# A split-float32 chain of products on one core: stationary operands laid out with a step of two, moving operands of three products read backwards

## Chip, cores and metric

The kernel runs on 1 core of a Trainium2 chip. The metric is the device time of one execution in microseconds; the median of three runs stands for the kernel. Engines are named as the profile names them: PE (TensorE, its matmuls), PEld (its weight loads), DVE (VectorE), ACT (ScalarE), POOL (GpSimd), SP (the queue that issues most transfers).

## What is computed

Three layers follow each other; batch 8, sequence 576, width 512, inner width 1024, all float32 (the weights of the feed-forward parts come as 64-bit floats and are brought to float32 on the chip).

```
q_s = softmax(q, -1);  k_s = softmax(k, over the sequence)
x   = q_s @ (k_s^T @ v)                                # linear attention, 8 heads of 64
gate = sigmoid(causal 5-tap convolution of x);  val = x @ w_val
y   = (gate * val) @ w_out
xk  = mu_k * y + (1 - mu_k) * y_prev;  xr likewise with mu_r
k   = relu(xk @ w_k);  v = (k * k) @ w_v;  r = sigmoid(xr @ w_r)
out = r * v
```

## The kernel before, in words

The 8 x 576 rows of the sequence are cut into 12 tiles of 384 columns (`T`), and features lie on the 128 partitions. Tile i goes through the steps V (`val`, with W_val), Y (`y`, W_out), R (`r`, W_r), and H and A alternating (`hid`, W_k; `vacc`, W_v): eight H steps, each A step three H steps behind its own (`LAG`, line 59). In V, Y and H a 128 x 128 block of the weight is the stationary operand and an activation of 384 columns the moving one (`product`, line 568). In R and A the roles are turned: a 128-column part of the activation is stationary and 512 columns of the weight move (lines 628 and 652).

Tile 0 multiplies in plain float32, and each of its products has two records in the trace. From tile 1 on, every operand a is split into a rounded part "hi" and a remainder "lo" in the format float32r (`split`, line 439: ACT casts the hi part, DVE subtracts for the lo part), and each product becomes three: hi x hi, and hi x lo and lo x hi (`passes`, line 446). Weights are split once, chunk by chunk, between tiles 0 and 1 (`split_weight`, line 228: ACT writes hi at line 240, DVE writes lo at line 241). The squared hidden activations are split by `hid` (lines 641 to 644) into a pair of tiles `kh`, `kl`, from eight buffers of one tag.

Every product has a weight load of its own; the load of the next product is recorded while the present one streams. In the compiled program of this kernel, each weight load is written with the address of its last column and a step of minus one element; each moving operand and each output has a step of plus one.

The order of the work is written out by hand: `FRONT` (line 22) for the first tiles, and from tile 2 on one side step list `REST` (line 38) that places the next tile's attention, convolution and rounds of k and v behind numbered steps of the present tile. The pads `LEFT_GAP` and `RIGHT_GAP` (line 56) shift where the pools lie.

Of the kernel before, what the change touches and what calls it, by code (L numbers as in the profile page):

```python
# [9 lines left out]
F32R = mybir.dt.float32r  # L10
# [56 lines left out]
def tile_linear_attention_gated_conv_channel_mix(  # L67
# [15 lines left out]
    nc = tc.nc  # L83
    B, H, S, D = q.shape
    DM = H * D
# [3 lines left out]
    P = 128  # L89
    NC = DM // P  # L90
    NF = DFF // P
    T = 384
# [9 lines left out]
    WC = 512  # L102
# [5 lines left out]
    work = ctx.enter_context(tc.tile_pool(name="work", bufs=1))  # L108
    gatep = ctx.enter_context(tc.tile_pool(name="gated", bufs=1))
# [17 lines left out]
    def f32(ap):  # L127
        return ap.bitcast(F32)
# [15 lines left out]
    def scratch(name):  # L144
        return work.tile([P, T], F32, tag="m", bufs=4, name=name)
# [43 lines left out]
    def tap(c, t):  # L189
# [6 lines left out]


    HALF = ("wout", "wv")
    SHAPES = {"wval": (w_val, DM, DM), "wout": (w_out, DM, DM), "wr": (w_r, DM, DM), "wk": (w_k, DM, DFF), "wv": (w_v, DFF, DM)}
    CHUNKS = {  # L200
        f"{w}{x}": (w, at) for w, (_, rows, width) in SHAPES.items()
        for x, at in enumerate((kc, c0) for c0 in range(0, width, WC) for kc in range(rows // P))
    }
    PLACES = len(CHUNKS) + 1
    raws, whole, upper, lower = {}, {}, {}, {}

    def place(dtype, name):
        return wts.tile([P, WC], dtype, tag="w", bufs=PLACES, name=name)

    def load_weight(n):  # L210
        w, (kc, c0) = CHUNKS[n]
        here = n in LEFT_WEIGHTS
        raw = raws[n] = (first if here else early).tile([P, WC, 2], U32, tag="raw", bufs=1 if here else 6, name="raw")
        nc.sync.dma_start(raw.rearrange("p n w -> p (n w)"), SHAPES[w][0][kc * P:(kc + 1) * P, 2 * c0:2 * (c0 + WC)])

# [5 lines left out]
    def open_upper():  # L221
        pool = ctx.enter_context(tc.tile_pool(name="upper", bufs=1))
        for w in ("wk", "wv"):
            _, rows, width = SHAPES[w]
            t = pool.tile([P, rows // P, width], F32R, name=f"{w}_hi")
            upper.update({(w, kc): t[:, kc, :] for kc in range(rows // P)})

    def split_weight(n):
        w, (kc, c0) = at = CHUNKS[n]
        if (w, kc) not in upper:  # L230
            if w in ("wk", "wv"):
                first_ctx.close()
                open_upper()
            else:
                pair = early.tile([P, 2, WC], F32R, tag="raw", bufs=6, name=f"{w}_hi")
                upper.update({(w, kc // 2 * 2 + x): pair[:, x, :] for x in range(2)})
        h, t = upper[w, kc][:, c0:c0 + WC], whole[at]
        l = lower[at] = place(F32R, "lower")
        scale = 0.5 if w in HALF else 1.0
        nc.scalar.activation(h, t, AF.Copy, scale=scale)  # L240
        nc.vector.scalar_tensor_tensor(out=l, in0=t, scalar=scale, in1=f32(h), op0=ALU.mult, op1=ALU.subtract)

    def weight(i, w, kc, c0, n):

        at = w, (kc, c0 // WC * WC)
        o = c0 % WC
        if i == 0:
            return (whole[at][:, o:o + n],)
        return upper[w, kc][:, c0:c0 + n], lower[at][:, o:o + n]


    kvs = []
# [178 lines left out]
    def pair_of(tag, bufs, pool=work):  # L431
        return lambda name: tuple(pool.tile([P, T], F32R, tag=tag, bufs=bufs, name=name + x) for x in "hl")

    x_pair, g_pair, q_pair, k_pair = pair_of("x", 8), pair_of("g", 8, gatep), pair_of("q", 2), pair_of("k", 8)

    def one(tag, bufs, name):
        return (gatep if tag == "g" else work).tile([P, T], F32, tag=tag, bufs=bufs, name=name)

    def split(a, pair):

        nc.scalar.copy(pair[0], a)  # L441
        nc.vector.tensor_sub(pair[1], a, f32(pair[0]))  # L442
        return pair

    def passes(po, left, right, start, stop, turn=False):

        m = ((0, 0),) if len(left) == 1 else ((0, 0), (0, 1), (1, 0)) if turn else ((0, 0), (1, 0), (0, 1))
        for x, (a, b) in enumerate(m):
            nc.tensor.matmul(  # L449
                po, lhsT=left[a], rhs=right[b], start=start and x == 0, stop=stop and x == len(m) - 1  # L450
            )

    def padded(i, h, tag, bufs, name, pool=odd):

# [41 lines left out]
    def x_chunk(st, i, c):  # L496
        segs = segments(i)
        g = len(segs)
        px = ps_w.tile([P, 512], F32, tag="w", name="px")
        for o, n, b, s in segs:  # L500
            kv = (kvf[b],) if i < 2 else kvs[b % 2]
            passes(px[:, o:o + n], tuple(a[:, c, :] for a in kv), tuple(a[:, o:o + n] for a in st["q", c]), True, True)
        xv = padded(i, HALO, "xf", 2, "xf") if i else padded(i, HALO, "xf", NC, "xf", first)
        data = xv[:, :, HALO:]
        fill_past(i, xv, tail_x[:, c, :])
        nc.scalar.copy(data, px[:, :T].rearrange("p (g t) -> p g t", g=g))
        keep_tail(i, xv, tail_x[:, c, :])
        st["xv", c] = xv
        if i == 0:
            st["x", c] = (xv[:, 0, HALO:],)  # L510
            return
        xh, xl = st["x", c] = x_pair("x")
        gx = lambda a: a.rearrange("p (g t) -> p g t", g=g)
        nc.scalar.copy(gx(xh), data)
        nc.vector.tensor_sub(gx(xl), data, gx(f32(xh)))
# [38 lines left out]
    def main_steps(i, xs):  # L554
# [3 lines left out]
        st = {}  # L558
        gx = lambda a: a.rearrange("p (g t) -> p g t", g=g_n)

        def bank(pool, tag, name):
            return pool.tile([P, 512], F32, tag=tag, name=name)
# [4 lines left out]

        def product(po, w, at, acts):
            for c, a in enumerate(acts):
                passes(po, weight(i, w, c, at, P), a, c == 0, c == NC - 1)  # L570

        def row(po, w, c, a):

            for m in range(NC):
                passes(po[m][:, :T], weight(i, w, c, m * P, P), a, c == 0, c == NC - 1)

        def val(m):
            if i == 0:
                if m == 0:
                    st["pv"] = four("pv")  # L580
                row(st["pv"], "wval", m, xs["x", m])
                return
            pv = bank(ps_w, "w", "pv")
            product(pv[:, :T], "wval", m * P, [xs["x", c] for c in range(NC)])
            gated(m, pv)
# [8 lines left out]
        def y(c):  # L594
            if i == 0:
                if c == 0:
                    st["py"] = [bank(ps_w, "w", "py") if m < 2 else bank(ps_acc, "acc", "py") for m in range(NC)]
                row(st["py"], "wout", c, st["g", c])
                return
            py = bank(ps_w, "w", "py")  # L600
            product(py[:, :T], "wout", c * P, [st["g", m] for m in range(NC)])
            keep_y(c, py)
# [18 lines left out]
        def part(pair, t):  # L621
            return tuple(a[:, t * P:(t + 1) * P] for a in pair)

        def r(c):
            if c == 0:
                st["r"] = [bank(ps_acc, "acc", f"racc{t}") for t in range(NT)]
            for t in range(NT):
                passes(st["r"][t], part(st["xr", c], t), weight(i, "wr", c, 0, DM), c == 0, c == NC - 1, True)

        def rsig():  # L630
            for t in range(NT):
# [6 lines left out]
        def hid(f):  # L638
            ph = bank(ps_w, "w", "ph")
            product(ph[:, :T], "wk", f * P, [st["xk", c] for c in range(NC)])  # L640
            rf = one("k", 8, "rf") if i == 0 else scratch("rf")
            nc.scalar.activation(rf, ph[:, :T], AF.Relu)  # L642
            nc.scalar.activation(rf, rf, AF.Square)
            st["k", f] = (rf,) if i == 0 else split(rf, k_pair("k"))

        def vacc(fs, ts):

            if fs[0] == 0:
                st["v"] = [bank(ps_acc, "acc", f"vacc{t}") for t in range(NT)]
            for f in fs:  # L650
                for t in ts:
                    passes(st["v"][t], part(st["k", f], t), weight(i, "wv", f, 0, DM), f == 0, f == NF - 1, True)
            if fs[-1] == NF - 1 and len(ts) == NT:
                for t in ts:
                    finish(t)

        def finish(t):
            rs = st["rs", t]
            nc.vector.scalar_tensor_tensor(
                out=rs, in0=rs, scalar=1.0 if i else 0.0, in1=st["v"][t], op0=ALU.add, op1=ALU.mult  # L660
            )
            r0 = i * T + t * P
            nc.sync.dma_start(out[r0:r0 + P, :], rs)
# [85 lines left out]
    for n in CHUNKS:  # L749
        todo_front["l" + n] = lambda n=n: load_weight(n)  # L750
        todo_front[n] = lambda n=n: decode_weight(n)
        todo_front["s" + n] = lambda n=n: split_weight(n)
# [55 lines left out]
```

## Time and profile before

| | us |
|---|---|
| median of 3 runs | 812.47 (812.2 to 812.85) |
| span of the profiled execution | 810.1 |
| first split product (tile 1, step V) | 106.84 after the start |
| last product | 805.90 |

The profiled execution's span runs from its first instruction to its last; the median of the runs is 2.3 us longer. The page gives busy shares of engines, a picture of the span in 40 slices, and the chain of work that ended last. PE's busy time is modelled and matmuls overlap in it (one of 384 columns is recorded as 0.34 us long, while the next starts 0.17 us after it), so the pace of the products is read from starts, or from the chain, which counts each piece once.

### The profile page before, as it was taken

What the parts mean: (1) busy time and instruction counts of PE and PEld (TensorE: products, weight loads), DVE (VectorE), ACT (ScalarE), POOL (GpSimd) and SP (SyncE); (2) the same over time, 40 slices, a digit from 0 to 9 for tenths busy, and PEclk for the clock granted to TensorE, in tenths of its full rate; (3) what the DMA queues carried; (4) which work ended last, traced back from release to release, by engine and by line L of the source; (5) the groups of instructions that cost most, each with busy time, mean ns of one, the idle gap of its engine ahead of it and who ended that gap; (6) DMA issues with size and microseconds to landing.
All of it is one profiled execution on the core that took longest, in us unless ns stands there. A gap on an engine that the chain in (4) does not pass through costs nothing.

```text
span 810.1 us, 12242 instructions
## 1 busy us (share of the span) xinstructions
PE 798.3 (99%) x4578; PEld 701.2 (87%) x4578; DVE 564.5 (70%) x1016; ACT 479.3 (59%) x948; POOL 59.2 (7%) x224
## 2 busy tenths in 40 slices
PE   6999999999999999999999999999999999999998
PEld 5545588999999999989989999999999999998996
DVE  7999889976777577577758577577576747644611
ACT  4667678637746746655754763763764674664542
POOL 2130001000002001000000100100000100100000
PEclk9999999999999999999999999999999999999999
DMA  9786220132222102013041211211222010000001
GB/s 310 244 269 217 59 78 1 40 98 59 75 63 59 40 27 72 7 36 91 7 98 46 53 40 39 60 39 40 59 65 73 1 37 23 22 1 14 26 1 40
DMA packets 92537, 53.25 MB, mean 66 GB/s; under 512 B 74018, under 2 KB 84286, under 8 KB 92478
## 3 DMA queue, kind: packets, MB, share of 16 engines
q1 hardware_dynamic: 92432, 52.44, 22.3%
q8 instruction: 36, 0.59, 0.3%
q14 instruction: 23, 0.19, 0.1%
q10 hardware_dynamic: 46, 0.02, 0.0%
HBM read 43.02 MB, written 9.44 MB: 65 GB/s over the span
## 4 chain that ended last, share of the span: by engine, by line
PE 95%; DMA 2%; DVE 1%; ACT 1%; SPq 1%; issue 0%; ACTq 0%
PE ph L449 25%; PE vacc L449 25%; PE racc L449 12%; PE pv L449 12%; PE py L449 12%; PE px L449 4%; PE kvacc L347 2%; PE pq L476 2%; DMA raw<-in_moe_w_val_dram 1%; DMA raw<-in_moe_w_k_dram 1%; DVE gate L548 1%; DMA kt<-in_k_dram 1%; PE mx L333 0%; PE pmT L321 0%; SPq L303 0%; DVE whole L152 0%
## 5 line engine op out<-in xcount | busy, mean ns | idle before, releaser
L548 DVE SCALAR_TENSOR_TENSOR gate<-xf,cw,gate 128x384 f32<-128x384 f32 x192 | 117.2, 615 | 5.1 <-ACT gate L546 2.3
L449 PE MATMUL ph<-xkh,wk_hi 128*128 128x384 f32 x352 | 120.3, 342 | 0.0
L449 PE MATMUL ph<-xkl,wk_hi 128*128 128x384 f32 x352 | 118.3, 336 | 0.0
L449 PE MATMUL ph<-xkh,lower 128*128 128x384 f32 x352 | 118.1, 336 | 0.0
L642 ACT ACTIVATE rf<-ph 128x384 f32<-128x384 f32 x96 | 46.8, 488 | 99.0 <-PE ph L449 98.1
L449 PE MATMUL vacc<-wv_hi,kh 128*128 128x512 f32 x264 | 104.0, 394 | 0.0
L449 PE MATMUL vacc<-lower,kh 128*128 128x512 f32 x264 | 103.2, 391 | 0.0
L449 PE MATMUL vacc<-wv_hi,kl 128*128 128x512 f32 x264 | 103.1, 391 | 0.0
L442 DVE TENSOR_TENSOR kl<-rf,kh 128x384 fp32r<-128x384 f32 x88 | 48.9, 556 | 70.1 <-ACT kh L441 69.1
L616 DVE SCALAR_TENSOR_TENSOR xm<-yf,mus,xm 128x384 f32<-128x384 f32 x96 | 56.5, 614 | 24.2 <-ACT xm L615 23.7
L449 PEld LDWEIGHTS ph<-xkh,wk_hi 128*128 128x128 f32 x352 | 66.2, 188 | 2.0 <-ACT xkh L441 0.2
L449 PEld LDWEIGHTS ph<-xkh,lower 128*128 128x128 f32 x352 | 66.2, 188 | 1.9
L449 PEld LDWEIGHTS ph<-xkl,wk_hi 128*128 128x128 f32 x352 | 66.1, 188 | 0.0
L494 DVE TENSOR_TENSOR ql<-pq,qh 128x384 fp32r<-128x384 f32 x40 | 22.2, 556 | 62.5 <-ACT qh L493 62.5
L441 ACT CAST gh<-gf 128x384 fp32r<-128x384 f32 x44 | 22.5, 511 | 72.0 <-DVE gf L589 72.0
L449 PE MATMUL py<-gh,wout_hi 128*128 128x384 f32 x176 | 59.6, 343 | 0.0
L449 PE MATMUL pv<-xh,lower 128*128 128x384 f32 x176 | 59.5, 338 | 0.0
L449 PE MATMUL pv<-xh,wval_hi 128*128 128x384 f32 x176 | 59.5, 338 | 0.0
L449 PE MATMUL pv<-xl,wval_hi 128*128 128x384 f32 x176 | 59.3, 337 | 0.0
L449 PEld LDWEIGHTS vacc<-wv_hi,kl 128*128 128x128 f32 x264 | 49.5, 188 | 11.0 <-DVE kl L442 0.3
L449 PE MATMUL py<-gl,wout_hi 128*128 128x384 f32 x176 | 58.2, 339 | 0.0
L449 PE MATMUL py<-gh,lower 128*128 128x384 f32 x176 | 58.0, 338 | 0.0
(132 smaller groups left out, 1723.0 us busy)
## 6 DMA issues: line engine op xcount, KB each, us to landing
out_dram<-rs SPq DMA_DIRECT2D x36, 256.0 KB, 2.0
kt<-in_k_dram SPq DMA_DIRECT2D x16, 512.0 KB, 4.5
qt<-in_q_dram SPq DMA_DIRECT2D x29, 256.0 KB, 3.4
vt<-in_v_dram SPq DMA_DIRECT2D x56, 128.0 KB, 3.6
raw<-in_moe_w_k_dram SPq DMA_DIRECT2D x8, 512.0 KB, 5.5
raw<-in_moe_w_v_dram SPq DMA_DIRECT2D x8, 512.0 KB, 6.8
raw<-in_moe_w_val_dram SPq DMA_DIRECT2D x4, 512.0 KB, 6.3
raw<-in_moe_w_out_dram SPq DMA_DIRECT2D x4, 512.0 KB, 8.4
```

Source lines behind the costliest of these rows:

```text
L347: nc.tensor.matmul(acc[e * D:(e + 1) * D, x * VW:(x + 1) * VW], lhsT=kt[:, 2 * x + e, s, :], rhs=st["v"][:, 2 * x + e, s, :], start=(s == ...
L441: nc.scalar.copy(pair[0], a)
L442: nc.vector.tensor_sub(pair[1], a, f32(pair[0]))
L449: nc.tensor.matmul(po, lhsT=left[a], rhs=right[b], start=start and x == 0, stop=stop and x == len(m) - 1)
L476: nc.tensor.transpose(pq[:, t * P:(t + 1) * P], qt[:, t, 2 * c:2 * c + 2, :].rearrange("p h d -> p (h d)"), f32(ident))
L494: nc.vector.tensor_sub(ql, pq[:, :T], f32(qh))
L548: nc.vector.scalar_tensor_tensor(out=gx(gate), in0=xv[:, :, HALO - sh:HALO - sh + L], scalar=tap(c, HALO - sh), in1=gx(gate), op0=ALU.mult ...
L616: nc.vector.scalar_tensor_tensor(out=gx(xf), in0=yv[:, :, 1:], scalar=mu[:, c:c + 1], in1=gx(xf), op0=ALU.mult, op1=ALU.add)
L642: nc.scalar.activation(rf, ph[:, :T], AF.Relu)
```

## The change

Four things are altered, all for tiles 1 to 11; tile 0 keeps its products.

The split weights of W_val, W_out and W_k (`WOVEN`) keep their places in memory, but the 512 columns of a chunk are stored woven: column n of the first 256 lies at element 2n, column 256 + n at element 2n + 1. ACT and DVE write them so (lines 240 and 241, once), and a stationary block of 128 columns is then read with a step of two elements.

The pair `kh`, `kl` of the squares becomes one tile of 2T elements with hi in the even and lo in the odd elements, four buffers in place of eight. ACT writes hi and DVE writes lo with a step of two, and A's stationary blocks are read with a step of two. In tile 0 the same buffers hold two unsplit squares each, one behind the other.

The moving operands of the products with W_val, W_k and W_v (`BACK`) are read from the last column to the first, and the output in PSUM is written from the last column to the first as well, so that the result lies as before. W_out's and W_r's products keep their direction.

R's stationary operand stays dense.

```diff
+    BACK = ("wval", "wk", "wv")
+    WOVEN = ("wval", "wout", "wk")
+
+    def woven(a):
+
+        return a.rearrange("p (n e) -> p e n", e=2)
...
         scale = 0.5 if w in HALF else 1.0
+        if w in WOVEN:
+            h, l, t = woven(h), woven(l), t.rearrange("p (e n) -> p e n", e=2)
         nc.scalar.activation(h, t, AF.Copy, scale=scale)
...
-        return upper[w, kc][:, c0:c0 + n], lower[at][:, o:o + n]
+        pair = upper[w, kc][:, c0 - o:c0 - o + WC], lower[at]
+        if w in WOVEN:
+            return tuple(woven(a)[:, o // (WC // 2), o % (WC // 2):o % (WC // 2) + n] for a in pair)
+        return tuple(a[:, o:o + n] for a in pair)
...
+    def k_tile():
+        return work.tile([P, 2 * T], F32R, tag="k", bufs=4, name="k")
+
+    def k_pair():
+        t = k_tile().rearrange("p (t e) -> p e t", e=2)
+        return tuple(t[:, e, :] for e in range(2))
...
-    def passes(po, left, right, start, stop, turn=False):
+    def passes(po, left, right, start, stop, turn=False, back=False):
 
         m = ((0, 0),) if len(left) == 1 else ((0, 0), (0, 1), (1, 0)) if turn else ((0, 0), (1, 0), (0, 1))
+        back = back and len(left) > 1
+        o = po[:, ::-1] if back else po
         for x, (a, b) in enumerate(m):
-            nc.tensor.matmul(
-                po, lhsT=left[a], rhs=right[b], start=start and x == 0, stop=stop and x == len(m) - 1
-            )
+            r = right[b][:, ::-1] if back else right[b]
+            nc.tensor.matmul(o, lhsT=left[a], rhs=r, start=start and x == 0, stop=stop and x == len(m) - 1)
...
-                passes(po, weight(i, w, c, at, P), a, c == 0, c == NC - 1)
+                passes(po, weight(i, w, c, at, P), a, c == 0, c == NC - 1, back=w in BACK)
...
-            rf = one("k", 8, "rf") if i == 0 else scratch("rf")
+            if i:
+                rf = scratch("rf")
+            else:
+                if f % 2 == 0:
+                    st["rf"] = f32(k_tile())
+                rf = st["rf"][:, f % 2 * T:(f % 2 + 1) * T]
             nc.scalar.activation(rf, ph[:, :T], AF.Relu)
             nc.scalar.activation(rf, rf, AF.Square)
-            st["k", f] = (rf,) if i == 0 else split(rf, k_pair("k"))
+            st["k", f] = (rf,) if i == 0 else split(rf, k_pair())
...
-                    passes(st["v"][t], part(st["k", f], t), weight(i, "wv", f, 0, DM), f == 0, f == NF - 1, True)
+                    passes(st["v"][t], part(st["k", f], t), weight(i, "wv", f, 0, DM), f == 0, f == NF - 1, True, "wv" in BACK)
```

## Rows read from the trace of the kernel before

**Rows 1.** The page: engines, granted clock by slice, shares of the chain.

```profile
PE 798.3 (99%) x4578; PEld 701.2 (87%) x4578; DVE 564.5 (70%) x1016; ACT 479.3 (59%) x948; POOL 59.2 (7%) x224
PEclk9999999999999999999999999999999999999999
PE 95%; DMA 2%; DVE 1%; ACT 1%; SPq 1%; issue 0%; ACTq 0%
```

**Rows 2.** The chain, last tile, split products: start us, us, engine, output, count.

```profile
747.97 8.34 PE pv L449 x48
756.31 8.47 PE py L449 x48
764.78 8.17 PE racc L449 x36
...
781.25 2.08 PE ph L449 x12
783.33 2.05 PE vacc L449 x9
```

**Rows 3.** The chain, tile 0, plain float32 products, two records each.

```profile
88.36 2.58 PE ph L449 x8
...
91.92 2.58 PE vacc L449 x6
```

**Rows 4.** Groups of instructions, PE: output<-operands, shapes, count, busy us, mean ns.

```profile
L449 PE MATMUL ph<-xkh,wk_hi 128*128 128x384 f32 x352 | 120.3, 342 | 0.0
L449 PE MATMUL vacc<-wv_hi,kh 128*128 128x512 f32 x264 | 104.0, 394 | 0.0
L449 PE MATMUL py<-gh,wout_hi 128*128 128x384 f32 x176 | 59.6, 343 | 0.0
L449 PE MATMUL pv<-xh,lower 128*128 128x384 f32 x176 | 59.5, 338 | 0.0
```

**Rows 5.** The timeline, PE, narrow split products of x: start us, us recorded.

```profile
465.94 0.25 PE L449 MATMUL px<-qh,kv_hi 128*128 128x192 f32 x1
466.02 0.28 PE L449 MATMUL px<-qh,kv_lo 128*128 128x192 f32 x1
466.14 0.28 PE L449 MATMUL px<-ql,kv_hi 128*128 128x192 f32 x1
466.25 0.27 PE L449 MATMUL px<-qh,kv_hi 128*128 128x192 f32 x1
466.36 0.27 PE L449 MATMUL px<-qh,kv_lo 128*128 128x192 f32 x1
466.47 0.28 PE L449 MATMUL px<-ql,kv_hi 128*128 128x192 f32 x1
```

**Rows 6.** ACT's copies with stepped and with dense reads, and the split: ns min/median/max.

```profile
L488 ACT COPY q<-pq x4: 458/478/486, 17.2 to 29.3; 128x384 f32<-128x384 f32 x4
...
L486 ACT COPY q<-pq x4: 478/480/485, 85.8 to 101.6; 128x384 f32<-128x384 f32 x4
...
L441 ACT CAST kh<-rf x88: 498/514/536, 139.4 to 801.0; 128x384 fp32r<-128x384 f32 x88
L442 DVE TENSOR_TENSOR kl<-rf,kh x88: 547/557/562, 139.9 to 801.5; 128x384 fp32r<-128x384 f32 x88
```

**Rows 7.** Windows: step V in tiles 3, 4 and 10, then H and A in tile 7 (busy us).

```profile
236.68:245.25 8.57, 8.57 (x52) 8.54 (x50) 8.57 (x17) 1.56 (x3) 1.06 (x2) 1.00 0.24 92
300.68:309.46 8.78, 8.78 (x54) 8.70 (x53) 8.44 (x18) 2.07 (x4) 1.03 (x1) 1.00 0.23 91
686.34:694.66 8.32, 8.32 (x49) 8.32 (x48) 6.53 (x12) 2.06 (x4) 0.50 (x1) 1.00 0.25 97
...
520.38:556.88 36.50, 36.50 (x193) 33.48 (x192) 23.20 (x36) 22.39 (x46) 0.48 (x3) 1.00 0.10 22
```

**Rows 8.** The timeline, the last H's squares and the A products that wait for them.

```profile
801.52 0.56 DVE L442 TENSOR_TENSOR kl<-rf,kh 128x384 fp32r<-128x384 f32 x1 [3.57 <-ACT kh L441]
801.54 0.19 PEld L449 LDWEIGHTS vacc<-wv_hi,kh 128*128 128x128 f32 x1 [0.28 <-ACT kh L441]
...
802.14 0.30 PEld L449 LDWEIGHTS vacc<-wv_hi,kl 128*128 128x128 f32 x2 [0.30 <-DVE kl L442]
```

More of the change, by code (lines that the diff above doesn't have):

```diff
@@ L432, in pair_of @@
         return lambda name: tuple(pool.tile([P, T], F32R, tag=tag, bufs=bufs, name=name + x) for x in "hl")
-    x_pair, g_pair, q_pair, k_pair = pair_of("x", 8), pair_of("g", 8, gatep), pair_of("q", 2), pair_of("k", 8)
+    x_pair, g_pair, q_pair, k_pair = pair_of("x", 8), pair_of("g", 8, gatep), pair_of("q", 2), None
+    def k_tile():
[3 more added lines that the diff above has]
+        return tuple(t[:, e, :] for e in range(2))
     def one(tag, bufs, name):
@@ L627, in r @@
             for t in range(NT):
-                passes(st["r"][t], part(st["xr", c], t), weight(i, "wr", c, 0, DM), c == 0, c == NC - 1, True)
+                passes(st["r"][t], part(st["xr", c], t), weight(i, "wr", c, 0, DM), c == 0, c == NC - 1, True, "wr" in BACK)
         def rsig():
```

## The prediction

> **What bounds the kernel now.** I read the page first: PE is busy for 99% of the span, 95% of the chain that ended last is PE, and PE's granted clock is in the top tenth in every slice [rows 1], which is its upper level of 2.4 GHz. So no wait, transfer or clock decides; the number of products and the time from one product to the next do. That pace is read next, from the chain of the last tile, which nothing interrupts [rows 2]: V takes 8.34 / 48 = 173.8 ns a product, Y 8.47 / 48 = 176.5, R 8.17 / 36 = 226.9, H 2.08 / 12 = 173.3, A 2.05 / 9 = 227.8. At 2.4 GHz and one column a cycle 384 columns are 160.0 ns and 512 are 213.3; the two widths confirm it, since 226.9 - 173.3 = 53.6 ns for 128 more columns. So each split product pays about 13.3 ns beside its columns, at either width. Then tile 0 as the control [rows 3]: a plain float32 record takes 2.58 / 8 = 322.5 ns for 384 columns and 2.58 / 6 = 430 for 512, that is two cycles a column and 2.5 to 3.3 ns beside them. Plain products have a weight load each, as split ones do. Some 10.8 ns a product (13.3 - 2.5) therefore come only where columns stream at full pace.
>
> **What these 10.8 ns may be.** No row names them. What changes between the two is how densely the moving operand is read while the next weights are loaded. The narrow products of x show the load's own pace [rows 5]: at 192 columns (80 ns of streaming) starts lie 0.11 to 0.12 us apart, so a load takes about 110 ns for 128 elements, half the pace of a moving operand. Loads walk downwards through memory and moving operands upwards, as the compiled program has it. With the change the moving operand of V, H and A walks downwards too, and the load covers two elements of memory for each one that it takes: both then walk in one direction at one pace. If the 10.8 ns are the two streams getting in each other's way where they pass in the same part of the memory, V, H and A lose most of them. Y gets the step of two without the turn and keeps opposite directions.
>
> **The change part by part.** Counts from [rows 4], three groups a product: V 528, Y 528, H 1056, A 792; R is left alone.
>
> Pace of V, H and A: between 0 and 10.8 ns less a product if the change helps (the floor is the plain product's 2.5 ns), up to 10.8 more if the doubled reach of the load doubles the meetings. I take two thirds, 7.2 ns: the one place where the trace shows less than the usual 13 ns is the first narrow product behind a wide one, 0.08 us between starts against 80 ns of columns [rows 5], some 6 ns or less, which is nearer to two thirds gone than to nothing or all. V and H: 1584 x 7.2 = 11.4 us. A: 792 x 7.2 = 5.7 us.
>
> Pace of Y: one of the two conditions is met, so half of that, 3.6 ns (bounds 10.8 more to 10.8 less): 528 x 3.6 = 1.9 us.
>
> Writes with a step of two by ACT and DVE: weights once (16 of 28 chunks), squares 88 times. No row shows such a write. The nearest is ACT's copy that reads with a step of 128 elements: 478 ns, against 480 for the dense one of the same shape [rows 6]. I take nothing from there; the other end is a doubling (less than dense is excluded, as the dense writes run at the same pace as all others of their width). Doubled, kh and kl would add 0.51 and 0.56 us eight times a tile in a stage where DVE is busy 23.2 and ACT 22.4 of 36.5 us [rows 7], with A three H steps behind: hidden but in the last tile, where the chain would end 1.1 us later.
>
> One tile for kh and kl: a product that reads kh might now wait for kl as well. With three H steps between, that is hidden in every tile but the last, where PE already waits 0.28 us for kh and 0.30 us for kl [rows 8]; there it costs at most the two kh products that now run ahead, 0.46 us. The buffers hold as many squares as before, so none comes free later. No DMA moves.
>
> Given back: PE getting faster meets DVE in V. In eight of the eleven tiles (1 and 3 to 9) DVE is busy for nearly the whole of V, as in the first two windows of [rows 7]; in three it has 2 us to spare, as in the third. In the eight, V's 48 x 7.2 = 0.35 us may turn into a wait of Y for the gated activations: 8 x 0.35 = 2.8 us, and 0.3 for the end.
>
> Sum: 11.4 + 5.7 + 1.9 - 3.1 = 15.9 us. The profiled span of 810.1 becomes 794.2; the runs' median lies 2.3 us above the span, so 812.5 - 15.9 = **796.6 us**.
>
> **The rivals.**
> All of it goes: V, H, A and Y fall to the plain product's 2.5 ns: 2904 x 10.8 = 31.4, less 8 x 0.52 + 0.3 = 4.5 given back: 26.9 us, **786 us**. For it: the plain products stand at 2.5 ns in every clean group. Against: two things must fit, and Y meets only one.
>
> Nothing is gained: the 10.8 ns are a fixed cost of starting a product at full pace, say because a stream that is used as fast as it is fetched cannot run ahead. For it: the cost is the same for V, R and H, whose operands lie in different pools, 13 to 14 ns each [rows 2]; collisions might be expected to vary more. Against: Y and A stand above the others by 1 to 3 ns with the same shapes, so something varies. **811 us**. [...]
>
> Slower, by the load: a step of two makes the load touch twice the memory. If each visit costs and the direction does not matter, V, Y, H and A pay 10.8 ns more: 2904 x 10.8 = 31 us, **844 us**. Worse, if the load itself takes twice its 110 ns, 384-column products are bound by 220 in place of 174 ns: 2112 x 46 = 97 us, **910 us**, while A at 228 stays. It decides as soon as a load passes 174 ns, and shows first in Y, where nothing else is changed. Against it: loads of 110 ns leave 64 ns of room.
>
> Slower, by the output: descending writes to PSUM at half the pace would bring V, H and A to the plain products' 322 and 430 ns: 1584 x 149 + 792 x 202 = 396 us, **1209 us**. No row shows a descending write. [...]
>
> **How the numbers follow.** Forecast (two thirds, give or take a third; 788 to 806): 0.46. All of it: 0.17. Nothing: 0.17 (809 to 813), of which 0.05 with a gain of over 0.2%. Slower by the load's meetings: 0.10, spread from 818 to 844; by the load's length 0.05; by the output 0.05. The likeliest is the forecast, 796.6. About 0.2% (1.6 us) is what a measurement of this kernel can tell from no change. Faster 0.46 + 0.17 + 0.05 = 0.68; same 0.12; slower 0.20. The range of 782 to 832 leaves out half of the load's meetings (0.05), the two large losses (0.10) and a sliver below 782 (0.04).
>
> **What would show it.** In the chain of the last tile: V and H at 166 to 167 ns and A at about 220, R at 227 as before. Y between 170 and 176; Y is the step of two alone, so Y above 177 with V and H below 173 would say that the direction does the work, and Y as fast as V that the step does. V's window in the eight tiles: DVE full and Y waiting for gl. kh and kl at 0.51 and 0.56 us as before. V and H at 173 and A at 227 would make the prediction wrong by the fixed cost; anything near 220 in Y, by the load; 320 in V and H, by the output.

## The result and the profile after

The changed kernel takes 820.98 us, median of four runs (820.71 to 821.92); the kernel before took 812.34 us beside it (812.07 to 812.85). The ratio is 1.0109, interval 1.0094 to 1.0123: 1.1% slower, where 796.6 us was forecast. The profiled execution has a span of 818.7 us, 8.6 us more than before. One of the nine runs of the kernel before that stand beside the first four experiments took 1549.08 us at a mean granted clock of 0.903; the median of 811.83 us given there has it in (811.73 without it), the ratios do not.

The page after: busy us of each engine with its share of the span, the granted clock by slices, and the chain's shares by engine, to be held against [rows 1].

```profile
PE 807.4 (99%) x4578; PEld 713.9 (87%) x4578; DVE 565.6 (69%) x1016; ACT 483.7 (59%) x948; POOL 60.3 (7%) x224
PEclk9999999999999999999999999999999999999999
...
PE 96%; DVE 1%; DMA 1%; ACT 1%; issue 0%; ACTq 0%
```

The kernel is bound as before: PE is 99% busy and makes up 96% of the chain, the granted clock stays at its upper level (mean 1.000 of full speed, before 0.997), and there are as many products and loads as before. So the time can only have gone into the pace.

The chain of the last tile after (start us, us, engine, output, line, count), which answers to [rows 2]:

```profile
755.68 8.53 PE pv L470 x48
764.21 8.48 PE py L470 x48
772.68 8.19 PE racc L470 x36
...
789.29 2.11 PE ph L470 x12
791.40 2.10 PE vacc L470 x9
```

V rose from 8.34 to 8.53 us, H from 2.08 to 2.11, A from 2.05 to 2.10; Y (8.47 to 8.48) and R (8.17 to 8.19) hardly moved. A tile without interruption has eight H and eight A steps: from the first H to the last A the last tile takes 814.82 - 780.88 = 33.94 us, before 806.30 - 772.95 = 33.35. So H and A together cost 0.59 us a tile, V 0.19, Y and R 0.03. Times eleven split tiles: 6.5 + 2.1 + 0.3 = 8.9 us, against 8.6 us of span. That leaves no room for a new wait or transfer of any size.

Y's own change hides in this view. In the last tile both kernels wait once in Y (a gl product is recorded with 0.44 us before and 0.45 us after, where its neighbours have 0.34). The mean time from one product's start to the next one's in the same step, over the whole trace and with gaps of more than 1.1 times the median left out, shows each step's pace (ns):

```
              V      Y      R      H      A
before      173.8  173.3  227.2  173.4  228.8
after       177.7  175.1  227.6  175.5  233.9
```

By this table the loss is V 3.9 x 528 = 2.1, Y 1.8 x 528 = 1.0, H 2.1 x 1056 = 2.2, A 5.1 x 792 = 4.0 us and R 0.2: 9.5 us, 0.9 more than the span grew. Of this, 0.4 us are waits of Y for gh that became shorter (0.9 us before, 0.5 after); the rest was not followed up. The same measure is used below for the experiments.

One group of weight loads before (busy us, mean ns); then, after, groups of weight loads, of ACT's cast and DVE's subtraction for the squares, and then from the timeline the two loads that wait for the last squares:

```profile
L449 PEld LDWEIGHTS ph<-xkh,lower 128*128 128x128 f32 x352 | 66.2, 188 | 1.9
```

```profile
L470 PEld LDWEIGHTS ph<-xkh,lower 128*128 128x128 f32 x352 | 68.5, 195 | 1.8
L470 PEld LDWEIGHTS vacc<-lower,k 128*128 128x128 f32 x264 | 52.0, 197 | 6.9
L470 PEld LDWEIGHTS racc<-lower,xrh 128*128 128x128 f32 x132 | 24.8, 188 | 4.9
L459 ACT CAST k<-rf 128x384 fp32r<-128x384 f32 x88 | 49.2, 561 | 2.3
L460 DVE TENSOR_TENSOR k<-rf,k 128x384 fp32r<-128x384 f32 x88 | 49.1, 558 | 73.9 <-ACT k L459 73.6
```

```profile
809.97 0.19 PEld L470 LDWEIGHTS vacc<-wv_hi,k 128*128 128x128 f32 x1 [0.27 <-ACT k L459]
...
810.57 0.55 PEld L470 LDWEIGHTS vacc<-wv_hi,k 128*128 128x128 f32 x3 [0.28 <-DVE k L460]
```

A load with a step of two is recorded with 194 to 197 ns, a dense one (R) with 188, as the loads of all five split weights were before. ACT's stepped cast takes 561 ns on average where the dense one took 517, DVE's subtraction 558 where it took 556 ([rows 6] has the medians before, 514 and 557). The last A waits 0.27 and 0.28 us for its squares, as in [rows 8], so the tile that kh and kl share costs nothing.

### The profile page after: what moved, and what is told of

Same layout as the page of the kernel before. It is cut to its first block, busy times and chain, and to the rows that moved or that the text cites. A ratio compares the mean times of both kernels' runs of the same rounds, so it can differ in the third digit from the quotient of the medians.

```text
span 818.7 us, 12247 instructions
## 1 busy us (share of the span) xinstructions
PE 807.4 (99%) x4578; PEld 713.9 (87%) x4578; DVE 565.6 (69%) x1016; ACT 483.7 (59%) x948; POOL 60.3 (7%) x224
## 4 chain that ended last, share of the span: by engine, by line
PE 96%; DVE 1%; DMA 1%; ACT 1%; issue 0%; ACTq 0%
PE vacc L470 25%; PE ph L470 25%; PE pv L470 12%; PE racc L470 12%; PE py L470 12%; PE px L470 3%; PE kvacc L358 3%; PE pq L495 2%; DMA raw<-in_moe_w_k_dram 1%; DVE gate L567 1%; PE heat L762 1%; PE pmT L332 1%; PE mx L344 0%; DVE whole L152 0%; DVE raw L151 0%; DVE gf L608 0%
## 5 line engine op out<-in xcount | busy, mean ns | idle before, releaser
L470 PE MATMUL vacc<-wv_hi,k 128*128 128x512 f32 x528 | 180.1, 400 | 0.0
L470 PEld LDWEIGHTS vacc<-wv_hi,k 128*128 128x128 f32 x528 | 103.8, 197 | 17.6 <-DVE k L460 0.3
L470 PE MATMUL vacc<-lower,k 128*128 128x512 f32 x264 | 104.9, 398 | 0.0
L460 DVE TENSOR_TENSOR k<-rf,k 128x384 fp32r<-128x384 f32 x88 | 49.1, 558 | 73.9 <-ACT k L459 73.6
L666 ACT ACTIVATE rf<-ph 128x384 f32<-128x384 f32 x88 | 43.1, 491 | 95.5 <-PE ph L470 94.6
L470 PEld LDWEIGHTS ph<-xkh,wk_hi 128*128 128x128 f32 x352 | 68.6, 195 | 1.9
L470 PEld LDWEIGHTS ph<-xkh,lower 128*128 128x128 f32 x352 | 68.5, 195 | 1.8
L470 PEld LDWEIGHTS ph<-xkl,wk_hi 128*128 128x128 f32 x352 | 68.5, 195 | 0.0
L470 PEld LDWEIGHTS vacc<-lower,k 128*128 128x128 f32 x264 | 52.0, 197 | 6.9
```

Of the source, the lines that this page charges most:

```text
L470: nc.tensor.matmul(o, lhsT=left[a], rhs=r, start=start and x == 0, stop=stop and x == len(m) - 1)
```

## The experiments

Unless another base is named, each kernel is the one before with an edit in `passes`, for split products of all five weights; `l`, `r` and `o` stand for stationary, moving and output. A kernel that was timed once stands beside a run of the kernel before on the same chip. The kernel before itself was timed between 810.7 and 812.9 us but for that one run, so a difference under some 2 us is read from the pace of the products and not from the time.

**The two halves of the change.** The theory after the result: one half, the direction of reading or the step of the loads, costs more than the other gains. First the step without the turn, an edit of the kernel after:

```
-    BACK = ("wval", "wk", "wv")
+    BACK = ()
```

> The changed kernel without the reversal: stationary operands of V, Y, H and A keep their step of two, every moving operand and output walks forwards again. If the step of two alone costs the time, the last tile keeps V at 178 ns a product, H at 176 and A at 234, and the kernel stays at about 820 us. If the reversal costs it, V, H and A go back to 174, 173 and 228 ns and the time to 812 to 813 us; the weight loads stay at about 195 ns in both. If the two only work together (loads and moving operands meeting in step), neither value holds and V, H and A fall below 173 or lie between.

817.86 us, ratio 1.0077 (1.0063 to 1.0092). Then the turn without the step, in the products of W_val, W_k and W_v:

```
+            if on:
+                r, o = r[:, ::-1], o[:, ::-1]
```

> The kernel before with the reversal alone: moving operands and outputs of V, H and A walk backwards, stationary operands are dense and the squares lie in a pair of tiles. If the reversal alone costs the time: about 820 us, V 178, H 176, A 234 ns, loads at 188 ns. If the step of two costs it: 812 us and 174, 173, 228 ns. If the stationary load and the moving operand meet less in one direction: below 812 us, with V and H under 173 ns.

819.84 us, ratio 1.0102 (1.0088 to 1.0117). Parts of their chains in the last tile, first the step alone, then the turn alone:

```profile
752.97 8.32 PE pv L470 x48
...
786.30 2.12 PE ph L470 x12
788.42 2.10 PE vacc L470 x9
```

```profile
754.87 8.53 PE pv L454 x48
...
786.41 2.10 PE vacc L454 x9
788.51 2.12 PE ph L454 x12
```

Both halves lose. The turn alone costs V 8.53 - 8.34 = 0.19 us, or 4 ns a product; the step alone leaves V where it was (8.32), so V's whole loss in the changed kernel is the turn's. H and A lose to either: by the mean pace H 1.6 ns to the step and 3.1 to the turn, A 3.9 and 4.6, and Y 1.5 to the step. The two do not add up: 6.0 us and 8.0 us alone, 8.6 together; in A the pace goes from 228.8 to 232.7, to 233.4, and with both to 233.9. Why the second half finds so little left was not settled. The kernel with the step alone also has the tile that kh and kl share; what part of A's 3.9 ns is the tile's was not separated.

**Is it reading or writing backwards?** The turn changes both ends of a product. These two kernels turn only one end, so output columns are permuted.

```
+                r = r[:, ::-1]
```

> The kernel before with the moving operand read backwards and the output written forwards, in all five products (the columns of each product come out in the wrong order). If the reading direction costs: V, Y, H at 176 to 180 ns and A and R at about 233, and the time some 10 us above the kernel before. If the writing direction costs: all products as before, 174, 176, 173, 227, 228 ns, and 812 us.

```
+                o = o[:, ::-1]
```

> The kernel before with the output written backwards and the moving operand read forwards, in all five products (the columns of each product come out in the wrong order). If the writing direction costs: V, Y, H at 176 to 180 ns and A and R at about 233, some 10 us above the kernel before. If the reading direction costs: 812 us with every product as before.

Reading backwards in all five: 824.21 us (before 811.83). Writing backwards in all five: 812.07. Chains of the last tile, reading first:

```profile
758.80 8.53 PE pv L454 x48
767.34 8.59 PE py L454 x48
775.93 8.40 PE racc L454 x36
```

```profile
747.79 8.34 PE pv L454 x48
756.13 8.47 PE py L454 x48
764.61 8.17 PE racc L454 x36
...
779.02 2.05 PE vacc L454 x9
781.07 2.08 PE ph L454 x12
```

Writing downwards repeats [rows 2] row by row: it is free. Reading downwards costs V, H and A as much as the turn did (by the mean pace 177.8, 176.4 and 233.4 ns, with the turn 177.8, 176.5 and 233.4), and now Y (8.47 to 8.59) and R (8.17 to 8.40, 6 ns a product) too. Its 12.4 us are 4.4 more than the turn in three weights, and Y and R account for them: 3.4 x 528 + 6.2 x 396 = 4.2 us.

**Which order costs?** Reading `r` in groups of four elements (16 bytes): first with the groups from last to first and each group read forwards, then with rising groups and each read backwards. Output columns are permuted in both.

```
+                r = r.rearrange("p (n e) -> p n e", e=4)[:, ::-1, :]
```

> The kernel before with the moving operands of all five products read in groups of four elements (16 bytes), the groups from last to first, the four of a group forwards (columns come out in another order). If reading backwards costs because the stream walks down through memory, this costs what the full reversal cost: 176 to 178 ns and 233, about 824 us. If it costs because elements of one group are taken in falling order, this is as before: 173 to 174 and 227 to 229 ns, 812 us.

```
+                r = r.rearrange("p (n e) -> p n e", e=4)[:, :, ::-1]
```

> The kernel before with the moving operands of all five products read in groups of four elements, the groups from first to last, the four of a group backwards (columns come out in another order). If falling order within a group costs: 176 to 178 and 233 ns, about 824 us. If walking down costs: as before, 812 us.

825.0 us and 812.29 us. Y and R in the last tile, in that order:

```profile
768.22 8.59 PE py L454 x48
776.81 8.40 PE racc L454 x36
```

```profile
756.49 8.48 PE py L454 x48
764.96 8.17 PE racc L454 x36
```

The first is the reading backwards over again, the second the kernel before. So the loss lies in falling 16-byte groups, and the order within a group does not matter. Whether the unit that has to rise is 16 bytes or a larger one was not tried.

**Are the 10.8 ns meetings with the load?** Here stands the prediction's own mechanism. A load that reads the same column 128 times touches almost no memory, and one of 72 columns is shorter. Both compute other values; the second also leaves out 56 output rows in one of three products.

```
+                l = l[:, 0:1].to_broadcast([P, P])
```

> The kernel before, but each stationary operand of the split products is one column repeated 128 times (step of zero), so that a load touches 4 bytes of memory a partition and the products are not the reference's. If the 10 to 13 ns that a split product pays beside its columns come from loads and moving operands meeting in memory, they go: V, Y, H to 163 to 167 ns, A and R to 216 to 220, time about 785 us. If they are a fixed cost of starting a product at full pace: 173 and 227 ns as before, 812 us, and loads at 188 ns.

```
+                if x == 1:
+                    l, o = l[:, 0:72], o[0:72, :]
```

> The kernel before, but the middle one of each three split products has a stationary operand of 72 columns in place of 128 (and writes 72 rows; the rest of its sum is left out), so that one load in three is 47 ns shorter. If the 10.8 ns of a product come from the load and the moving stream running at once, the product that streams while the short load runs pays 72/128 of it: 168 to 169 ns in place of 173 in H and V, 222 in place of 227 in A and R. If they belong to the fetch of the moving operand alone, all three stay at 173 and 227 ns. The load itself should be recorded at some 142 ns.

815.51 us (before 811.43) and 814.57 us (before 811.18): neither is faster. With one column, the last tile:

```profile
751.02 8.40 PE pv L454 x48
...
767.89 8.34 PE racc L454 x36
...
788.72 2.08 PE ph L454 x12
```

With short loads, the group of loads concerned and pieces of the chain (V, R and three H steps):

```profile
L455 PEld LDWEIGHTS ph<-xkh,lower 128*72 128x72 f32 x352 | 49.8, 142 | 2.3
```

```profile
749.92 8.53 PE pv L455 x48
...
766.91 8.28 PE racc L455 x36
775.19 6.23 PE ph L455 x36
```

With one column per load H stays at 2.08 us, V and R rise (by the mean pace R from 227.2 to 231.5 ns, and A from 228.8 to 231.3), and nothing falls. With short loads V and R rise too, to 8.53 and 8.28 us, and H is 6.23 / 36 = 173.1 ns. The product that streams beside the load that is 188 - 142 = 46 ns shorter is hi x hi: by the mean pace it takes 173.9 ns in V, 173.9 in H and 229.5 in R, where it took 173.8, 173.1 and 227.2 before. If the load's path through memory or its length set the 10.8 ns, they would have shrunk in one of the two kernels. So what the load reads can add to the pace, but taking its path or its length away takes nothing off. Loads that walk upwards, and products without a load of their own, were not tried.

**Is it the moving operand's own reading?** The counterpart: the moving operand stays in one place. All kernels of this part but the last two compute other values.

```
+                r = r[:, 0:1].to_broadcast([P, r.shape[1]])
```

> The kernel before, but each moving operand of the split products is its first column repeated (step of zero), so that the stream touches 4 bytes a partition and the products are not the reference's. If the 10 to 13 ns come from how the moving operand is fetched (meeting the load, or fetched no faster than it is used), they go: 163 to 167 ns and 216 to 220, about 785 us. If they are a fixed cost of the product that has nothing to do with the memory: 173 and 227 ns, 812 us.

784.45 us (before 811.43), the only large gain of the study. The last tile:

```profile
723.19 7.84 PE pv L454 x48
731.03 8.10 PE py L454 x48
739.12 7.79 PE racc L454 x36
...
754.74 1.96 PE ph L454 x12
756.71 1.95 PE vacc L454 x9
```

V is 7.84 / 48 = 163.3 ns, R 216.4: 53.1 ns for 128 more columns, 0.415 ns a column, where the widths in [rows 2] give 53.6 / 128 = 0.419. The 160.0 and 213.3 ns that the prediction counts as columns are 0.4167 ns each, between the two. Beside them stand 3.3 and 3.1 ns, about what a plain product pays (2.5 and 3.3, [rows 3]). The whole 10 to 12 ns have gone, with every load as it was. By the mean pace V gains 10.4 x 528 = 5.5, Y 9.8 x 528 = 5.2, R 10.8 x 396 = 4.3, H 9.7 x 1056 = 10.2, A 12.2 x 792 = 9.7 us: 34.9, of which 27.0 arrive. Part of the other 8 us shows in PE's waits (us in total, times, longest), first before, then here:

```profile
PEld pmT L321 <- DVE pm L314: 2.7, 1, 2.7
...
PEld py L449 <- ACT gh L441: 0.9, 4, 0.3
```

```profile
PEld pmT L322 <- DVE pm L315: 6.7, 8, 2.8
...
PEld py L454 <- ACT gh L442: 2.6, 6, 0.5
```

How large may the place be? The first n columns, read again and again: 4 (16 bytes), 8 (32), 16 (64), 64 (256) and 128 (512 bytes).

```
+                r = r[:, 0:n].rearrange("p (o n) -> p o n", o=1).to_broadcast([P, r.shape[1] // n, n])
```

> The kernel before with the first four columns (16 bytes) of each moving operand read over and over (the products are not the reference's). If the cost comes with the change of groups, it goes as it went with one column: 162 and 216 ns, about 784 us. If it comes with the change of elements, it stays: 173 and 227 ns, 812 us.

> The kernel before with the first eight columns (32 bytes) of each moving operand read over and over (the products are not the reference's). If the cost comes with every change of a 16-byte group: 173 and 227 ns, 812 us. If the memory serves 32 bytes at a time: 162 and 216 ns, about 784 us.

> The kernel before with the first 16 columns (64 bytes) of each moving operand read over and over (the products are not the reference's). If the cost sets in as soon as the stream must fetch again and again: 173 and 227 ns, 812 us. If it grows with the stretch that is crossed: 162 to 166 and 216 to 220 ns, 785 to 792 us.

> The kernel before with the first 64 columns (256 bytes) of each moving operand read over and over (the products are not the reference's). If the cost sets in as soon as the stream must fetch again and again: 173 and 227 ns, 812 us. If it grows with the stretch that is crossed: half of it, 168 and 221 ns, about 800 us.

> The kernel before with the first 128 columns of each moving operand read three or four times over (the products are not the reference's), so that a stream touches 512 bytes a partition in place of 1536 or 2048, but at the full pace. If the 10.8 ns are the price of starting a stream of many bytes, paid once a product: 173 and 227 ns, 812 us. If they are paid for each new stretch of memory that the stream walks through, they fall to about a third in V, Y and H and a quarter in A and R: 166 and 219 ns, about 788 us.

In this order 786.2, 784.92, 844.07, 811.47 and 812.89 us (before 811.11 to 811.71). H in the last tile, for 64 and for 256 bytes:

```profile
811.93 2.18 PE ph L454 x12
```

```profile
780.50 2.08 PE ph L454 x12
```

Within 32 bytes the cost is gone. From 256 bytes on it is the same as in the whole operand, so how far the operand reaches does not matter. At 64 bytes it is higher than in the whole: V 183.2 ns and A 242.1, that is 23 and 29 ns beside the columns.

Last, two orders with the output columns in the same order, so that the product is unchanged: all even 16-byte groups and then all odd ones; and groups from the two halves of the operand in turn.

```
+                r, o = (t.rearrange("p (n a e) -> p a n e", a=2, e=4) for t in (r, o))
```

> The kernel before with the moving operands of all five products read by groups of four elements (16 bytes), even groups first and then the odd ones, rising; the output is written in the same order. If the cost beside the columns is per visit of a longer stretch of memory (32 bytes or more), it grows: 180 ns and more, 235 and more. If it is a start that rising order keeps small: 173 and 227 ns, 812 us. If neighbouring groups stand in each other's way, less than 173 and 227.

```
+                r, o = (t.rearrange("p (h n e) -> p n h e", h=2, e=4) for t in (r, o))
```

> The kernel before with the moving operands of all five products read by groups of four elements, one from the first half and one from the second half of the columns in turn; the output is written in the same order. If it only matters that each group is new: 173 and 227 ns, 812 us. If falling steps between groups cost (every second step falls by 752 bytes or more): 176 to 180 and 233 ns, 820 to 830 us. If neighbouring groups stand in each other's way, less than 173 and 227.

818.89 us (before 811.11) and 870.19 us. R in the last tile, in that order:

```profile
770.94 8.39 PE racc L454 x36
```

```profile
818.91 9.03 PE racc L454 x36
```

Even and odd apart costs the 512-column products 4 to 6 ns (R 227.2 to 233.1, A 228.8 to 232.6) and the 384-column ones under 1. Alternating halves cost 15 to 17 ns at 384 columns and 24 at 512. The output is written in the same scattered order in both; writing downwards was free, but scattered writing was not tried alone, so a part of these prices may be the writing's. Of the orders that read the whole operand none is faster than the rising one of the kernel before.

**What a larger step of the load does.** Columns of the stationary operand taken four apart in V, Y and H, three apart in R and A; the values differ.

```
-        return upper[w, kc][:, c0:c0 + n], lower[at][:, o:o + n]
+        if n == WC:
+            return upper[w, kc][:, c0:c0 + n], lower[at][:, o:o + n]
+        return tuple(a[:, o // P::WC // P] for a in (upper[w, kc][:, c0 - o:c0 - o + WC], lower[at]))
...
-            return tuple(a[:, t * P:(t + 1) * P] for a in pair)
+            return tuple(a[:, t * P:(t + 1) * P] if i == 0 else a[:, t::NT] for a in pair)
```

> The kernel before with stationary operands read from the dense tiles at a step of four elements in V, Y and H and of three in R and A (the output's order is wrong, nothing else changes). Steps of two lengthened the load by some 6 ns, from 188 to 194. If the load pays for the memory that it covers, it grows in proportion: about 207 ns at a step of four, 200 at three; A and R then at 233 to 240 ns and V, Y, H at 175 to 180. If a step of two is the end of what comes free (two elements out of each 16 bytes), the load breaks away at four: 250 ns and more, and V, Y and H are bound by it, above 200 ns. If the step matters only by its direction to the moving operand, nothing changes beyond the step of two: 174 to 175 and 233.

947.8 us. Loads of H (step four) and R (step three), then the chain of the last tile:

```profile
L451 PEld LDWEIGHTS ph<-xkh,lower 128*128 128x128 f32 x352 | 114.9, 327 | 0.0
L451 PEld LDWEIGHTS racc<-lower,xrh 128*128 128x128 f32 x132 | 33.3, 253 | 0.0
```

```profile
871.79 11.14 PE pv L451 x48
...
894.13 8.48 PE racc L451 x36
...
913.07 2.74 PE ph L451 x12
```

Only what the loads read was changed, and V takes 11.14 / 48 = 232 ns where it took 173.8: at step four the load sets the pace. With 188 ns dense, 194 at two, 253 at three and 327 at four, the knee lies beyond the step of two that the change uses. The load is 6 ns longer at two, 65 and 139 ns longer at three and four; why it grows so is not shown.

## Why the prediction was wrong

**What bounds it** was right: the time is set by PE's pace, and the measured paces give the measured loss (8.9 us by the chain, 8.6 by the span). Of the clock the profile gives the granted share alone, 0.997 before and 1.000 after; the 2.4 GHz and the one column a cycle of the prediction stand for the pace that the widths show, 128 columns in 53.6 ns [rows 2], which is 2.39 a nanosecond.

**The 10.8 ns** were sized rightly and put down to the wrong thing; this is the step that failed. The prediction took them for meetings of the load, walking down, with the moving operand, walking up, and expected two thirds back where both walk one way. The runs show that nothing of the cost goes when the load's path or length does (H at 173 ns with one column and with 72), and that only 3 to 4 ns are left beside the columns when the moving operand stays within 32 bytes. They tie the cost to the moving operand's own reading; a share of the load that neither its path nor its length changes is not excluded, since every product kept a load. So the gains of 11.4 us (V and H), 5.7 (A) and 1.9 (Y) had nothing to come from: the paces show losses of 4.3, 4.0 and 1.0 us in their place. The size of two thirds was taken from a narrow product of x [rows 5], which the change does not touch, so that row could not speak for the turn. That loads walk downwards is read from the compiled program; no run here shows it in the time.

**The turn** was given a price from zero to a gain, by itself; a loss was allowed only for the load's doubled reach. By itself it measures +4 ns in V, +3 in H and +5 in A: falling 16-byte groups. No rival named it. The change turned the reading as well as the writing; the writing had its rival, since no row showed a descending write, and the reading had none, though no row showed that either.

**The step of two** was in the rival of the load's meetings, at 10.8 ns in each of V, Y, H and A and 844 us (spread from 818). The measured 821 us lies in that spread, but by another sum: the step costs V nothing, Y and H 1.5 to 1.6 ns, A 3.9, in all 6.0 us alone. The load's doubled length, the next rival, is what a step of four does, with 232 ns in V; at step two the load grows by 6 ns, and V, with 173.5 ns, does not slow down. The prediction had a load decide as soon as it passes 174 ns; dense loads are recorded with 188 beside V's 173.8 and do not. Why A, H and Y feel a load that is still hidden is open.

**The output's direction**: the rival of 1209 us is out, since downward writes in all five steps give 812.07 us. The halved pace in its sum was the author's estimate, and no run shows it: with every output written downwards V stays at 8.34 and A at 2.05 us in the last tile, the values of [rows 2]. Whether a scattered write is slow was not tried alone.

**The rival of no gain** came nearest in its reason: a fixed cost that neither the load's path nor its direction changes. It erred by the 9 to 10 us between its 811 and the result, since the order of reading is not free. The 811 itself lies 1.5 us below the 812.5 that no gain would leave, and no row was given for that. Its objection, that Y stands 3 ns above the rest, was a misreading: the 8.47 us of [rows 2] hold one wait of Y for a gl, and Y's pace is 173.3 ns, like V's and H's. A does stand 1.6 ns above R.

**What was costed at nothing** was nothing: ACT's stepped cast is some 45 ns longer and hidden, DVE's is unchanged, the shared tile adds no wait at the end (0.27 and 0.28 us), R stays within 0.4 ns. The 3.1 us given back never came into play. With a gain of 10 ns or more in all five steps about 8 us are given back, in part to the waits of Y for the gated activations as the prediction had it, but that had 4.5, for four steps of the five.

**What stays open**: what the 10 ns are. They do not grow in proportion to the width (10.4 in V, 10.8 in R), which looks like a cost at each product's start; the excess of the 64-byte walk over the single column grows about as the width does (H 181.1 - 163.7 = 17.4, V 183.2 - 163.4 = 19.8; R 241.2 - 216.4 = 24.8, A 242.1 - 216.6 = 25.5), which looks like a cost of each visit. Whether the places in memory that follow one another too soon are the cause is argued by the orders that lose (falling, every second group, halves in turn, 64 bytes again), and not shown.

## What to carry to other kernels

Where PE's pace sets the time, a change of layout or of reading order is worth nanoseconds times thousands of products, so it is measured first, one end of the product at a time: turn the reading, turn the writing, step the load, each alone. Read a moving operand in rising order (read downwards in all five steps it cost 12.4 us here), leave the direction of the output free (812.07 us written downwards, 811.83 before), and keep the step of a float32 stationary operand at one, or at most two (6.0 us for two, with the shared tile; 947.8 us in all at four and three). A cost that no row names is not yet a cost that a new layout removes: a kernel that takes the suspected partner away (one column per load) tells it in one run.

## What the runs showed of the hardware

- A split product pays 13 to 16 ns beside its columns (taken at 0.4167 ns each) when the moving operand is read in rising order over 256 bytes or more, and 3 to 4 ns when it stays within 32 bytes. A single column in place of the whole operand was worth 27 us of 811 (784.45).
- Falling 16-byte groups cost 3 to 6 ns a product (825.0 us in all five steps); falling elements within them cost nothing (812.29 us), nor does a falling output (812.07).
- The same 64 bytes read over and over are slower (844.07 us) than the same 256 (811.47) or the same 32 (784.92).
- The load of 128 float32 columns is recorded with 188, 194, 253 and 327 ns at steps of one, two, three and four.
